# Gated linear attention with a feed-forward stage: the first nine units load groups of four tokens in long runs and turn them with 64-column products

## The chip, the cores and the metric

The kernel runs on one core of a Trainium2 chip. A core has a matrix engine (TensorE, PE in the profile, with PEld for its weight loads), a vector engine (VectorE, DVE), a scalar engine (ScalarE, ACT), a general engine (GpSimd, POOL) and a queue engine (SyncE, SP), which here issues all DMA transfers of data. PE writes its results to the accumulator memory PSUM, of which a bank holds 512 fp32 numbers per partition; all other data on the chip lies in SBUF with 128 partitions. The metric is the device time of one execution in microseconds (us); lower is better.

## What is computed

Two layers one after the other. First gated linear attention: for 4 batches, 8 heads, 768 tokens and 48 channels a head, a state of 48x48 is scaled by alpha row by row, gets the product of k and v added, and is read by q. Its output, 3072 tokens of 384 channels, goes through a feed-forward layer with 2048 hidden channels and a leaky maximum. All is fp32, except the two weight matrices, which arrive as float64.

```python
# q, k, v, alpha: (4, 8, 768, 48); alpha between 0.8 and 1.0
state = np.zeros((B, H, D, D), dtype=np.float32)
for t in range(S):
    state = alpha[:, :, t, :, None] * state + np.einsum('bhd,bhe->bhde', k[:, :, t], v[:, :, t])
    y[:, :, t] = np.einsum('bhd,bhde->bhe', q[:, :, t], state)
x = np.ascontiguousarray(y.transpose(0, 2, 1, 3)).reshape(B * S, H * D)   # 3072 x 384
h = x @ w_in                                                            # 384 x 2048
g = np.maximum(0.01 * h, h)
out = (g @ w_out).astype(np.float32)                                     # 2048 x 384
```

## The kernel before

**Units.** The 768 tokens are cut into 6 blocks of 128, and a *unit* is one block of one batch: 24 units, the block the slow index and the batch the fast one, so that units 0 to 3 are the first block of the four batches and carry no state in. The feed-forward layer takes three units at a time (`UPB = 3`). The first nine units, `AHEAD = 9`, run ahead of it; the other 15 are woven into it.

**One unit.** For the products the channels of two heads have to lie on partitions, 48 of one head at partition 0 and 48 of the other at 64 (`HB = 64`), and the 128 tokens along the row; four such pairs of heads make 512 columns, a bank of PSUM. alpha is turned into this layout and multiplied up along the tokens by a scan (`pc`, L309, one scan per pair); from the reciprocals of pc at every sixteenth token (L311) a second scan, backwards over all 512 columns, makes `rc` (L315). q times pc is `qs` (L334), k times rc is `ks` (L342). Eight products give the scores (L351); ACT copies them out (L361) and POOL zeroes the part above the diagonal (L362). ks is turned back to tokens on partitions (L374, copied by ACT, `ktok`). The outputs are products with the state (only from the second block on, units 4 and later) and with v (both L390); `kv` (L411) is what the unit adds to the state, copied by ACT for the first block (L430) or added to the state by DVE (L432). ACT and DVE split the outputs into two reduced-precision fp32 halves, high (L419) and low (L420), the input of the feed-forward layer.

**How the first nine units load and turn.** `load` puts tokens on partitions (`by_token`): each packet is the 48 channels of one token and head, 192 bytes, and a load of 192 KB has 1024 of them. alpha of unit 0 is loaded as two halves. A row then holds 8 heads at a pitch of 64, of which 48 are data; the gaps of 16 are filled with ones once, by DVE, at the start. `transposed` makes four PE transposes of 128x128 out of it (L272, against the unit matrix `ident`), one per pair of heads, into a whole bank. Later units load groups of four tokens, 768 bytes, and are turned by DVE in 32x32 blocks (L284); that stays as it is. There are two buffers each for alpha, q and k and three for v, so a load for unit u + 2 is issued when unit u has been turned.

**Order.** The program is written as a loop over units, in which `attention` interleaves the parts of unit u and of unit u + 1 (scans of u + 1; scores, mask and turned k of u; q and k of u + 1; outputs and state of u). Within the dependences the order on each engine is chosen by a scheduler from its own estimate of times; `tc.issue_after` ties single instructions to others. The PSUM banks of attention are two rings of three, `a` and `b`. PE keeps busy at the start with fillers, products of no use (`keep_warm`, L162, and `keep_warm_wide`, L167, which reads a tile of zeros): six ahead of everything, and some behind the turns of unit 0.

**Weights.** They arrive as 64-bit words in `raw` buffers on the same SP queue (L202, L206; the first two are tied to the v loads of units 4 to 7) and are converted by ACT and DVE into two fp32 halves (L237 to L257). The first of these jobs on ACT (L238) stands in ACT's order among the work of units 4 and 5; the conversions proper begin after ks of unit 7. With the feed-forward products (L487 in, L512 out, each a sum of three products of halves) PE is then supplied to the end.

## Time and profile before

| | |
|---|---|
| time, three runs | median 538.94 us (538.92 to 539.31) |
| profiled execution | 538.77 us, its span 537.1 us |
| PE busy | 518.8 us, 97% of the span; mean granted clock 0.991 |
| DVE, ACT, POOL busy | 375.0 us (70%), 234.0 us (44%), 49.1 us (9%) |
| instructions | 10383 |
| DMA | 92985 packets, 46.67 MB; 57856 of the packets under 512 bytes |

An engine's busy time is the time in which it executes; waits, and the issuing of transfers, are not in it. The span runs from the first to the last instruction. The granted clock is the share of full speed that the power throttle allowed PE. Most of the packets, and nearly all those under 512 bytes, are loads of attention; of 24 units' loads of v all are in 192-byte runs, of alpha, q and k those of the first nine units.

### The profile page before, as it was taken

The numbers are of one execution on the slowest core, as the hardware profiler recorded it, in microseconds if no ns is written. First come the engines' busy times: TensorE is split into PE (matmuls) and PEld (weight loads), VectorE is DVE, ScalarE is ACT, GpSimd is POOL, SyncE is SP. The second block draws the span as 40 slices with busy tenths as digits, with TensorE's granted clock in tenths as the row PEclk, the third lists the DMA queues.
The fourth block names the chain that finished last, engine by engine and source line by source line (L and its number), as shares of the span: only waits on it lengthen the run. The fifth ranks groups of instructions, "written<-read, shape, count | busy, mean of one in ns | idle before, by whom it ended". The sixth has DMA issues, their size and how long they took to land.

```text
span 537.1 us, 10383 instructions
## 1 busy us (share of the span) xinstructions
PE 518.8 (97%) x3934; PEld 492.6 (92%) x3934; DVE 375.0 (70%) x703; ACT 234.0 (44%) x514; POOL 49.1 (9%) x116
## 2 busy tenths in 40 slices
PE   8879899999999999999999999999999999999995
PEld 7668789999999899999999999999999999999995
DVE  6778999999988897875675685775777534332331
ACT  2665755555533453435334443344343354233331
POOL 3333510000000011010000001000000000000000
PEclk9999899999999999999999999999999999999998
DMA  9999854454823643533323422523201010001001
GB/s 149 163 179 183 198 140 119 117 131 136 183 53 87 190 117 78 107 81 98 70 67 70 108 69 64 98 50 92 71 0 38 11 35 1 22 1 45 1 1 49
DMA packets 92985, 46.67 MB, mean 87 GB/s; under 512 B 57856, under 2 KB 90112, under 8 KB 92928
## 3 DMA queue, kind: packets, MB, share of 16 engines
q1 hardware_dynamic: 92928, 45.93, 39.0%
q8 instruction: 33, 0.54, 0.4%
q14 instruction: 24, 0.20, 0.1%
HBM read 38.83 MB, written 4.72 MB: 81 GB/s over the span
## 4 chain that ended last, share of the span: by engine, by line
PE 86%; DVE 4%; DMA 3%; issue 2%; ACT 1%; SPq 1%; POOL 1%; ACTq 0%; DVEq 0%; POOLq 0%
PE ph L487 36%; PE b L512 32%; PE a L390 5%; PE a L351 4%; PE a L512 4%; DMA small<-in_alpha_dram 2%; DMA raw<-in_moe_w_in_dram 1%; PE a L374 1%; PE b L272 1%; PE a L411 1%; PE b L390 1%; DVE pc L309 1%; PE b L411 1%; POOL sm L362 1%; DVE rc L315 0%
## 5 line engine op out<-in xcount | busy, mean ns | idle before, releaser
L487 PE MATMUL ph<-large,w 128*128 128x384 f32 x1152 | 227.4, 340 | 2.8 <-DVE t L493 2.8
L487 PEld LDWEIGHTS ph<-large,w 128*128 128x128 f32 x1152 | 201.9, 189 | 5.5 <-DVE t L493 3.9
L512 PE MATMUL b<-w,gh 128*128 128x384 f32 x672 | 170.0, 340 | 0.0
L493 DVE TENSOR_TENSOR t<-ph,t 128x384 f32<-128x384 f32 x128 | 70.5, 551 | 88.7 <-ACT t L490 88.4
L512 PEld LDWEIGHTS b<-w,gh 128*128 128x128 f32 x672 | 119.7, 188 | 2.2 <-issue 0.5
L490 ACT ACTIVATE t<-ph 128x384 f32<-128x384 f32 x128 | 62.6, 489 | 130.1 <-PE ph L487 122.8
L495 ACT CAST gh<-t 128x384 fp32r<-128x384 f32 x128 | 65.7, 514 | 112.8 <-DVE t L493 102.6
L512 PE MATMUL b<-w,gl 128*128 128x384 f32 x336 | 107.4, 336 | 0.0
L499 DVE TENSOR_TENSOR gl<-t,gh 128x384 fp32r<-128x384 f32 x128 | 70.8, 553 | 34.4 <-ACT gh L495 33.2
L512 PEld LDWEIGHTS b<-w,gl 128*128 128x128 f32 x336 | 62.5, 188 | 0.1
L362 POOL TENSOR_SCALAR_AFFINE_SELECT sm<-sm 128x512 f32<-128x512 f32 x33 | 22.8, 705 | 113.3 <-ACT sm L361 113.3
L351 PE MATMUL a<-qs,ks 48*128 48x128 f32 x312 | 30.9, 287 | 0.1
L351 PEld LDWEIGHTS a<-qs,ks 48*128 48x128 f32 x312 | 25.9, 189 | 5.4 <-issue 4.4
L284 DVE STREAM_TRANSPOSE ks<-small 128x512 f32<-128x512 f32 x15 | 16.6, 1121 | 12.3 <-PE a L374 12.3
L390 PE MATMUL a<-sm,small 128*48 128x128 f32 (+1 forms) x312 | 23.2, 282 | 0.1
L319 POOL COPY pe<-pc 128x4 f32<-128x4 f32 x24 | 4.8, 202 | 188.6 <-DVE pc L309 188.6
L309 DVE TENSOR_TENSOR_SCAN pc<-e,small 128x128 f32<-128x128 f32 x60 | 20.1, 398 | 0.5 <-ACT pc L327 0.5
L367 POOL TENSOR_TENSOR small<-us,pe 112x192 f32<-112x192 f32 x20 | 11.9, 594 | 90.2 <-DVE us L432 87.5
L390 PEld LDWEIGHTS a<-sm,small 128*48 128x48 f32 (+1 forms) x312 | 17.1, 132 | 3.2 <-issue 3.0
L361 ACT COPY sm<-a 128x512 f32<-128x512 f32 x24 | 14.0, 585 | 13.8 <-PE b L351 11.1
L512 PE MATMUL a<-w,gh 128*128 128x384 f32 x96 | 20.0, 336 | 0.0
L315 DVE TENSOR_TENSOR_SCAN rc<-e,small 128x511 f32<-128x511 f32 x15 | 19.0, 1270 | 0.2
(86 smaller groups left out, 525.4 us busy)
## 6 DMA issues: line engine op xcount, KB each, us to landing
raw<-in_moe_w_out_dram SPq DMA_DIRECT2D x16, 384.0 KB, 3.9
small<-in_v_dram SPq DMA_DIRECT2D x24, 192.0 KB, 4.0
raw<-in_moe_w_in_dram SPq DMA_DIRECT2D x32, 144.0 KB, 3.9
out_dram<-t SPq DMA_DIRECT2D x24, 192.0 KB, 1.9
small<-in_alpha_dram SPq DMA_DIRECT2D x32, 96.0 KB, 2.3
small<-in_q_dram SPq DMA_DIRECT2D x30, 96.0 KB, 2.2
small<-in_k_dram SPq DMA_DIRECT2D x30, 96.0 KB, 2.2
small<-in_alpha_dram SPq DMA_DIRECT2D x30, 80.0 KB, 2.3
```

The lines of the kernel that those rows point to most:

```text
L284: nc.vector.transpose(t.rearrange("r p (j t) -> r p t j", t=T4), src.rearrange("r p (t d) -> r p t d", t=T4)[:, :, :, 0:32],)
L309: nc.vector.tensor_tensor_scan(pc[:, p, :], aT[:, p, :], ones.broadcast_to([P, C]), 1.0, ALU.mult, ALU.mult)
L315: nc.vector.tensor_tensor_scan(flat[2][:, NP * C - 2::-1], flat[0][:, NP * C - 1:0:-1], flat[1][:, NP * C - 2::-1], last, ALU.mult, ALU.add)
L351: nc.tensor.matmul(ss[s][:, p, :], ks[lo:lo + D, p, :], qs[lo:lo + D, p, :], start=True, stop=True)
L362: nc.gpsimd.affine_select(out=sm[s], in_=sm[s], compare_op=ALU.is_ge, fill=0.0, base=0, pattern=[[0, NP], [1, C]], channel_multiplier=-1)
L390: nc.tensor.matmul(y[s][HB * c:HB * c + lhsT.shape[-1], p % 2, :], lhsT, rhs, skip_group_check=True, **kw)
L487: nc.tensor.matmul(ph, w_in_of(f, wn, g), xt[:, g, :], start=n == 0, stop=n == 3 * NG - 1)
L490: put(ordered, "ACT", lambda: nc.scalar.mul(t, ph, 0.01))
L493: put(ordered, "DVE", lambda: nc.vector.tensor_tensor(t, ph, t, ALU.max))
L495: put(ordered, "ACT", lambda: nc.scalar.copy(gh, t))
L499: made["gl", i, f] = put(ordered, "DVE", lambda: nc.vector.tensor_tensor(gl, t, gh.bitcast(F32), ALU.subtract))
L512: nc.tensor.matmul(po[j], gt[:, js], w_out_of(f, wn), start=f == 0 and n == 0, stop=f == NF - 1 and n == 2)
```

## The change

For the first nine units alpha, q and k come in one transfer each with runs of four tokens, 768 bytes, 256 of them per load. Partition j*4 + p of the buffer gets group j (four tokens) of the head pair p, and the two heads of the pair (the *halves*, s) lie behind each other in the row at the pitch of 208. What before was the transpose of a pair of heads is now, for each of the four tokens n of a group and for each half s, a product of 64 columns of the buffer with `turn`, a unit matrix whose columns are permuted so that pairs come out as the slow and groups as the fast index. A product's result is 64 partitions by 128 columns; it goes to the half's partitions (0 to 63 or 64 to 127) and to every fourth column of the bank, from n on. So a tensor takes eight products, two for each of the four tokens, in place of four transposes. The gaps that are filled at the start become one run of 16 behind each half (by DVE) and the rest of the row (by POOL); `turn` is made by POOL with one copy from `ident`. The two halves of alpha's first load become one transfer, and the wide fillers and their tile of zeros are gone: q's, k's and alpha's turns of unit 0 each have two plain fillers behind the second and the fourth token.

```diff
--- before.py
+++ after.py
@@ -83,8 +83,8 @@
             parts.append(part)
         return parts
 
-    ident, mask, ones, acc, seed, *rest = pieces(
-        "small", F32, (P,), (C,), (1,), (2 * NU,), (NP, C), *[(NP * D,)] * B, *[(DM,)] * NV, *[(NP * PITCH,)] * sum(NL)
+    ident, turn, mask, ones, acc, seed, *rest = pieces(
+        "small", F32, (P,), (P,), (C,), (1,), (2 * NU,), (NP, C), *[(NP * D,)] * B, *[(DM,)] * NV, *[(NP * PITCH,)] * sum(NL)
     )
     state, vals_sb, rest = rest[:B], rest[B:B + NV], rest[B + NV:]
     loads_sb = [[rest.pop(0) for _ in range(n)] for n in NL]
@@ -123,11 +123,10 @@
         ts = slice(tb * C, (tb + 1) * C)
         t, src = loaded(u, i), (alpha, q, k)[i]
         if u < AHEAD:
-            n = H if u or i else H // 2
-            for h in range(0, H, n):
-                nc.sync.dma_start(
-                    by_token(t)[:, h:h + n, 0:D], src[b, h:h + n, ts, :].rearrange("h t d -> t h d")
-                )
+            nc.sync.dma_start(
+                t[:, 0:2 * PITCH].rearrange("r (s n) -> r s n", s=2)[:, :, 0:RUN],
+                src[b, :, ts, :].rearrange("(p s) (j t) d -> j p s (t d)", s=2, t=T4),
+            )
             return
 
         for a in range(4):
@@ -151,8 +150,6 @@
 
     nc.vector.memset(seed, 0.0)
     nc.vector.memset(ones, 1.0)
-    zeros = cst.tile([P, 4 * C], F32R, name="zeros")
-    nc.gpsimd.memset(zeros.bitcast(F32), 0.0)
 
     idle = ps_h.tile([P, 512], F32, name="ph")
 
@@ -161,21 +158,20 @@
         for _ in range(n):
             nc.tensor.matmul(idle[:, 0:C], seed[:, 0, :], seed[:, 1, :], start=True, stop=True)
 
-    def keep_warm_wide(n):
-
-        for _ in range(2):
-            nc.tensor.matmul(idle[:, 0:n], zeros[:, 0:P], zeros[:, 0:n], start=True, stop=True)
-
     keep_warm(6)
+    def tails(t):
+        return t[:, 0:2 * PITCH].rearrange("r (s n) -> r s n", s=2)[:, :, RUN:]
+
     for i in (0, 1, 2):
         for t in loads_sb[i]:
-            nc.vector.memset(by_token(t)[:, :, D:], 1.0)
+            nc.vector.memset(tails(t), 1.0)
     for n in range(max(NL)):
         for i in range(3):
             if n < NL[i]:
                 load(n, i)
         load_values(n)
     make_identity(nc, ident)
+    nc.gpsimd.tensor_copy(turn.rearrange("r (p j) -> r p j", p=NP), ident.rearrange("r (j p) -> r p j", p=NP))
     nc.gpsimd.memset(mask, 1.0)
     nc.gpsimd.affine_select(
         out=mask, in_=mask, compare_op=ALU.is_ge, fill=0.0, base=0,
@@ -183,7 +179,7 @@
     )
     for i in (0, 1, 2):
         for t in loads_sb[i]:
-            nc.gpsimd.memset(t[:, H * HB:], 1.0)
+            nc.gpsimd.memset(t[:, 2 * PITCH:], 1.0)
 
 
     runs = [(0, D, 0, 1, D), (D, GAP, NG * D, NG, 1), (HB, D, NP * D, 1, D), (BR, GAP, (NP + NG) * D, NG, 1)]
@@ -267,18 +263,17 @@
 
         src = loaded(u, i)
         if u < AHEAD:
-            ps = banks4()
-            for p in range(NP):
-                last = nc.tensor.transpose(
-                    ps[:, p, :], by_token(src)[:, 2 * p:2 * p + 2, :].rearrange("t h d -> t (h d)"), ident
-                )
-                if u == 0 and p % 2:
+            ps = bank()
+            for n in range(T4):
+                for s in (0, 1):
+                    at = s * PITCH + n * D
+                    last = nc.tensor.matmul(
+                        ps[HB * s:HB * (s + 1), n::T4], src[:, at:at + HB], turn, start=True, stop=True, skip_group_check=True
+                    )
+                if u == 0 and n % 2:
                     with tc.issue_after(last.ins):
-                        if i == 2:
-                            keep_warm_wide(4 * C if p == 1 else 2 * C)
-                        else:
-                            keep_warm(2)
-            return ps
+                        keep_warm(2)
+            return ps.rearrange("r (p t) -> r p t", p=NP)
         t = atp.tile([P, NP, C], F32, name=name, **kw)
         src = src.rearrange("r (p n) -> r p n", p=NP)[:, :, 0:RUN]
         nc.vector.transpose(
```

The order that the scheduler makes of it changes as well. On SP, which issues the transfers, the start of the program stood like this (`in_alpha_dram`, `in_q_dram`, `in_k_dram` and `in_v_dram` are the inputs):

```order
L128 DMA small<-in_alpha_dram 128x4x48 x2
L128 DMA small<-in_q_dram 128x8x48
L128 DMA small<-in_k_dram 128x8x48
L128 DMA small<-in_alpha_dram 128x8x48
L128 DMA small<-in_q_dram 128x8x48
L128 DMA small<-in_k_dram 128x8x48
L147 DMA small<-in_v_dram 128x8x48 x3
```

and now:

```order
L146 DMA small<-in_v_dram 128x8x48 x2
L126 DMA small<-in_alpha_dram 128x2x192
L126 DMA small<-in_q_dram 128x2x192
L126 DMA small<-in_k_dram 128x2x192
L126 DMA small<-in_alpha_dram 128x2x192
L126 DMA small<-in_q_dram 128x2x192
L126 DMA small<-in_k_dram 128x2x192
L146 DMA small<-in_v_dram 128x8x48
```

The first two loads of v have moved ahead of the first alpha.

On PE, one cycle of the early units from the turned-back k of a unit u on (the L272 behind it are q and k of unit u + 1, the lone one further down is alpha of unit u + 2):

```order
L374 MATMUL a<-small,ks 128x112 x4
L272 MATMUL b<-small 128x128 x4
L272 MATMUL a<-small 128x128 x4
L390 MATMUL b<-sm,small 64x128
L390 MATMUL b<-sm,small 48x128
L390 MATMUL b<-sm,small 64x128
L390 MATMUL b<-sm,small 48x128
L272 MATMUL b<-small 128x128 x4
L411 MATMUL b<-small,ktok 64x48
```

and the same cycle now, with the lines moved up by some four or five (L369 is the former L374, L270 the turns, L385 the former L390, L406 the former L411):

```order
L369 MATMUL a<-small,ks 128x112 x4
L270 MATMUL a<-small 64x128 x2
L270 MATMUL b<-small 64x128 x8
L270 MATMUL a<-small 64x128 x6
L385 MATMUL b<-sm,small 64x128
L385 MATMUL b<-sm,small 48x128
L385 MATMUL b<-sm,small 64x128
L385 MATMUL b<-sm,small 48x128
L270 MATMUL b<-small 64x128
L406 MATMUL b<-small,ktok 64x48
```

The first of alpha's eight products stands where all of alpha's transposes stood; its other seven have moved behind the kv products (L406) and the second half of the outputs, right ahead of the next scores.

On DVE, one unit of the early ones (the `x` halves, L420, belong to the unit before the one whose scans stand around them):

```order
L309 SCALAR_TENSOR_TENSOR pc<-b,small 128x128 x4
L310 MEMSET b 128x32
L420 TENSOR_TENSOR large<-b,large 112x2x128
L311 RECIPROCAL small<-pc 128x32
L420 TENSOR_TENSOR large<-a,large 112x2x128
L315 SCALAR_TENSOR_TENSOR rc<-b,small 128x511
L334 TENSOR_TENSOR qs<-b,pc 128x512
L342 TENSOR_TENSOR ks<-a,rc 128x512
```

and now (L415 is the former L420, L304 the scans over pc, L310 the scan over rc, L329 and L337 qs and ks):

```order
L415 TENSOR_TENSOR large<-a,large 112x2x128
L415 TENSOR_TENSOR large<-b,large 112x2x128
L304 SCALAR_TENSOR_TENSOR pc<-b,small 128x128 x4
L305 MEMSET b 128x32
L306 RECIPROCAL small<-pc 128x32
L310 SCALAR_TENSOR_TENSOR rc<-b,small 128x511
L329 TENSOR_TENSOR qs<-b,pc 128x512
L337 TENSOR_TENSOR ks<-a,rc 128x512
```

Both x halves of the unit before have moved ahead of the scans. (The names of the operations are the program's; the profile calls the scans TENSOR_TENSOR_SCAN.)

## The prediction

> **What bounds the kernel now.** I read the page, then busy time by stage, then the timeline of the first 60 us, since the change touches only units 0 to 8.
>
> ```profile
> span 537.1 us, 10383 instructions
> PE 518.8 (97%) x3934; PEld 492.6 (92%) x3934; DVE 375.0 (70%) x703; ACT 234.0 (44%) x514; POOL 49.1 (9%) x116
> PE ph L487 36%; PE b L512 32%; PE a L390 5%; PE a L351 4%; PE a L512 4%; DMA small<-in_alpha_dram 2%; DMA raw<-in_moe_w_in_dram 1%; PE a L374 1%; PE b L272 1%; PE a L411 1%; PE b L390 1%; DVE pc L309 1%; PE b L411 1%; POOL sm L362 1%; DVE rc L315 0%
> ```
>
> The span is 537.1 us of an execution of 538.77 us; the median of the runs is 538.94, 0.17 above. The chain is PE's. By stage (start:end, length, then busy time of PE, PEld, DVE, ACT, POOL, then the granted clock):
>
> ```profile
> 51.09:76.41 25.32, 22.74 (x234) 19.62 (x231) 24.16 (x42) 14.26 (x32) 9.19 (x11) 0.93 0.77 173
> 76.41:537.10 460.69, 453.05 (x3192) 436.61 (x3192) 312.18 (x568) 192.98 (x416) 22.82 (x56) 1.00 0.30 73
> ```
>
> From 76.41 on PE is full (453.05 of 460.69), and nothing there is edited. From 51.09, where ks of unit 7 is done, to 76.41 DVE is full (24.16 of 25.32) with weight conversions. So the end moves by as much as ks of unit 7 moves, less what DVE's 1.2 us of idle time can take back. What sets that moment is the pace of units 0 to 7, from one score product (L351) to the next:
>
> ```profile
> 5.69 1.36 DVE L309 TENSOR_TENSOR_SCAN pc<-a,small 128x128 f32<-128x128 f32 x4 [3.36 <-PE a L272]
> 10.00 0.37 PE L351 MATMUL a<-qs,ks 48*128 48x128 f32 x1
> 16.08 0.37 PE L351 MATMUL a<-qs,ks 48*128 48x128 f32 x1
> 32.92 0.37 PE L351 MATMUL a<-qs,ks 48*128 48x128 f32 x1
> 41.50 0.58 PE L351 MATMUL a<-qs,ks 48*128 48x128 f32 x1
> 47.13 0.37 PE L351 MATMUL a<-qs,ks 48*128 48x128 f32 x1
> ...
> 50.41 0.68 DVE L342 TENSOR_TENSOR ks<-a,rc 128x512 f32<-128x512 f32 x1
> ```
>
> These are the scores of units 0, 1, 4, 5 and 6 and the last ks: 6.08 us for unit 0, (32.92-16.08)/3 = 5.61 for units 1 to 3, 8.58 for unit 4, 5.63 for unit 5, then 3.96 to 51.09. Unit 4 is long because ACT, in order, waits for weights:
>
> ```profile
> ACT raw L238 <- DMA raw<-in_moe_w_in_dram: 2.6, 1, 2.6
> 30.95 2.84 SPq L202 DMA_DIRECT2D raw<-in_moe_w_in_dram  x4
> 37.14 0.66 PE L272 MATMUL b<-small 128*128 128x128 f32 x4 [1.99 <-ACT us L430]
> 39.10:42.50 3.40, 3.40 (x40) 3.31 (x39) 3.17 (x8) 1.37 (x5) 0.37 (x2) 0.50 1.30 148
> ```
>
> After 1.99 us without work PE also gets half the clock (0.50) for 3.4 us.
>
> **The change part by part.** *Transfers.* 192-byte packets become 768-byte ones. Two stretches, packets, MB, share of the 16 engines, of 12 us from 6 and of 9 us from 138:
>
> ```profile
> q1 hardware_dynamic: 10741, 2.03, 142.6%
> q1 hardware_dynamic: 2425, 1.52, 68.4%
> ```
>
> 192 KB in the first kind take 12 x 0.197/2.03 = 1.16 us of a full queue. In the second, with 640- and 768-byte packets, 9 x 0.684 x 0.197/1.52 = 0.80 if 100% is full and 0.56 if 142.6% is; I take 0.65. So 27 loads free some 13 us of transfer time. That would pay only where a unit waits for data: unit 0, unit 2 (1.24 us in unit 0's 6.08) and the weights of unit 4.
>
> *Order on SP.* Both v loads now stand ahead of the first alpha. Issues and landings (start and length; then, in the chain, a load from issue to landing):
>
> ```profile
> 0.82 0.99 SPq L128 DMA_DIRECT2D small<-in_alpha_dram  x2
> 3.03 4.60 DMA small<-in_alpha_dram
> small<-in_alpha_dram SPq DMA_DIRECT2D x1, 96.0 KB, 2.4
> small<-in_alpha_dram SPq DMA_DIRECT2D x1, 96.0 KB, 2.7
> ```
>
> The two halves land at 3.2 and 4.0, and alpha of unit 1, three loads later, at 7.63: (7.63-4.0)/3 = 1.2 each, in order of issue. So v of unit 0 lands at 4.0, of unit 1 at 5.2, and alpha at 5.85: 1.85 later than now. Bounds: 0 later if the queue let it pass, 2.0 later with 0.80 per load. I take the queue, since every landing shows it. POOL's new turn table is ready by then: its fills of 416 instead of 320 columns add 0.6 us, the copy perhaps 0.4, the dropped zeros give back 0.5, and they ended at 4.0. SP's waits for DVE's fills of the gaps end before the v issues do. q and k land 0.65 apart, ahead of their turns.
>
> *Turns.* Four transposes become eight 64-column products. Rows of one unit:
>
> ```profile
> 11.09 0.60 PE L374 MATMUL a<-small,ks 112*128 112x112 f32 x4
> 11.53 0.60 PE L272 MATMUL b<-small 128*128 128x128 f32 x4
> 11.97 0.60 PE L272 MATMUL a<-small 128*128 128x128 f32 x4
> 12.56 0.65 PE L390 MATMUL b<-sm,small 128*64 128x128 f32 x8
> ...
> 15.04 0.61 PE L411 MATMUL b<-small,ktok 128*64 128x48 f32 x15
> ```
>
> Four transposes are 4 records: 11.97-11.53 = 0.44, 0.11 a step. L390's four 64-column fp32 products are 8 records (two per product) and take 0.65, no more than four steps and the last one's 0.27: neighbours of different column halves run side by side. A tensor is then 16 records in 8 steps, 0.87 instead of 0.44. Bounds: 0.44 if a step could be halved, 1.74 if the halves did not pair. I take 0.87; L390 is the same shape. Per unit that is 3 x 0.43 = 1.3 us more on PE, which waits about 1.4 of each 5.61 us now, so the cover is just used up.
>
> *Pace.* From a score product: 1.53 to the turns (10.00 to 11.53); q and k 1.74, 3.27; L390 waits for rc, which frees its bank: the scan can start 0.25 after the scores and rc ends about 3.1 later, 3.4; four L390 0.44; the first of alpha's products, alone, 0.22; L411 and the other L390 1.04 (15.04 to 16.08); seven products 0.87. That is 5.95; I take 5.9, and 5.8 for unit 0, where that wait is nil. Units 4 and 5 have state products besides:
>
> ```profile
> 50.06 0.32 PE L390 MATMUL b<-qs,small 48*64 48x128 f32 x2
> ...
> 50.67 0.66 PE L272 MATMUL b<-small 128*128 128x128 f32 x4
> ```
>
> 0.61 more, while the wait for rc disappears and the alpha product is no longer alone: 6.2. DVE stays below: from the scan at 9.86 to the end of ks at 14.18 are 4.32, with L420 twice 5.05.
>
> ```profile
> 9.86 1.35 DVE L309 TENSOR_TENSOR_SCAN pc<-b,small 128x128 f32<-128x128 f32 x4
> 13.50 0.68 DVE L342 TENSOR_TENSOR ks<-a,rc 128x512 f32<-128x512 f32 x1
> ```
>
> DVE now does L420 ahead of the scan, so it waits for the two casts; but they end with L411, just before alpha's products, which the scan needs anyway: nothing. The old loop over us, state scaling and masks (5.61) falls away.
>
> *Sum.* Alpha 5.85; its products and two fillers to the scan 7.5 (now 5.69); reciprocal 9.3; the six fillers that wait for it (0.22 each), k's last product, two fillers and alpha of unit 1 take 3.0: scores of unit 0 at 12.3 instead of 10.0. Then 18.1, 24.0, 29.9, 35.8, 42.0, 48.2, and ks of unit 7 4.7 later (4.32, the state sum and a short wait) at 52.9 instead of 51.09. Unit 4's stall is gone in this: its weights follow v of unit 5, free at 28.9 instead of 30.0, and land near 33.5, where ACT comes at 33.8; if they take as long as now, up to 1 us returns. So +2.3 at the start, -0.3 unit 0, +0.9 units 1 to 3, -2.4 unit 4, +0.6 unit 5, +0.7 for the last step: +1.8. DVE's waits after 51 take back some 0.4: +1.4, or 538.77+1.4 = 540.2, 540.3 on the median's scale. The wide fillers were PE's waiting time; dropping them costs nothing.
>
> **Rivals.** Under 0.2% (1.08 us) nothing can be told from no change, so the bounds are 537.9 and 540.0.
>
> *Slow products.* Nine products of 384 columns at full rate (start, length):
>
> ```profile
> 76.41 1.83 PE ph L487 x9
> ```
>
> A step might double because results go into every fourth column, or the halves might not pair; no row writes PSUM with gaps. L390's pairs speak against the second. Price 2.6 us a unit over seven, 1.5 at the start: +20, 558 to 560. The Trainium skill, PSUM — Partial Sum Buffer, Specifications, says of PSUM's 8-byte cache lines that "any non-contiguous AP slows matmuls significantly"; by that rule this case would be the forecast, and no run here shows it yet. I hold it less likely since an fp32 step already takes 0.11 us for 128 columns while L487's wider ones take 1.83/9 = 0.20 for 384, so each column has time to spare.
>
> *Half clock at the start.* PE idles from 4.46 (end of the first fillers) to 5.85, 1.4 us. If that costs a 3.4 us window as in unit 4, the PE-bound piece before 12.3 takes 0.9 to 2.9 longer: 542.2. It decides if such a gap, 1.4, is enough; 1.99 was, and the 1.24 us wait for unit 2's alpha was not. The Trainium skill, TensorE: Matmul & The Clock Gate, Part 1, wants one whole idle window of about 3.4 us; by it this case cannot happen, but the trace's 1.99 disagrees.
>
> *No delay at the start.* If alpha passes the v loads it lands at 4.2, and 1.65 us come back: 538.6, no change. Against it is the even spacing of landings.
>
> *PE not the bound: faster.* If a 64-column product took half a step, PE would need 4.6 and DVE's 5.05 (5.35 with state) would set the pace: 0.85 x 5 units and 0.6 at the start, 4.9 in all: 535.3. It wins from a pace of 5.5 down. Against it, L390's steps.
>
> **How the numbers follow.** Forecast 51%, own range 538.6 to 542; no delay 17%; half clock 14%; slow products 10%; faster 8%. The range 536.9 to 543.6 leaves out the slow products and most of the fast case. Faster: 8, 5 from the forecast's lower edge, 4 from no delay: 17%. Same: 16 and 13: 29%. Slower: 30, 14 and 10: 54%.
>
> **What would show it.** Alpha's first product at 5.9 and the scores of unit 0 at 12.3; L270 in 8 steps of 0.11; score products 5.9 and 6.2 apart with PE never long idle; no long ACT wait for raw; ks of unit 7 near 52.9. I am wrong if the pace falls under 5.6, a step differs from 0.11, or alpha lands before 5.

## The result and the profile after

The changed kernel takes 545.10 us (median of four runs, 544.01 to 545.55) against 539.12 (538.92 to 539.53) for the kernel before: ratio 1.0104, 95% interval 1.0082 to 1.0127, so it is 6 us slower. The forecast had the sign right and the size wrong: 540.3, with a range that ended at 543.6.

The page of the execution after (545.24 us, its span, the busy times, the chain and the packets):

```profile
span 543.4 us, 11011 instructions
PE 530.6 (98%) x4262; PEld 505.3 (93%) x4262; DVE 375.3 (69%) x703; ACT 235.9 (43%) x514; POOL 49.1 (9%) x116
PE ph L482 36%; PE b L507 32%; PE a L385 5%; PE a L346 5%; PE a L507 4%; PE b L270 2%; PE a L270 2%; PE a L369 1%; DMA small<-in_alpha_dram 1%; PE a L406 1%; PE ph L159 1%; PE b L385 1%; DVE pc L304 1%; DMA raw<-in_moe_w_in_dram 1%; PE b L406 1%
DMA packets 72234, 46.69 MB, mean 86 GB/s; under 512 B 30192, under 2 KB 69360, under 8 KB 72176
```

The transfers did what the change says: 27,664 fewer packets under 512 bytes. PE has 328 more records (an fp32 product has two) and 11.8 us more busy time; DVE, ACT and POOL are busy for as long as before within 2 us. From the timeline (start, length, engine, line), the scores of units 0, 1, 4, 5 and 6 and ks of unit 7, which answer to the rows at 10.00, 16.08, 32.92, 41.50, 47.13 and 50.41 of before:

```profile
15.46 0.37 PE L346 MATMUL a<-qs,ks 48*128 48x128 f32 x1
21.30 0.37 PE L346 MATMUL a<-qs,ks 48*128 48x128 f32 x1
38.84 0.37 PE L346 MATMUL a<-qs,ks 48*128 48x128 f32 x1
45.44 0.37 PE L346 MATMUL a<-qs,ks 48*128 48x128 f32 x1
51.91 0.37 PE L346 MATMUL a<-qs,ks 48*128 48x128 f32 x1
55.72 0.68 DVE L337 TENSOR_TENSOR ks<-a,rc 128x512 f32<-128x512 f32 x1
```

And by stage (length, busy PE, PEld, DVE, ACT, POOL, granted clock, DMA share, GB/s):

```profile
15.46:21.30 5.84, 5.84 (x102) 5.41 (x100) 4.75 (x11) 3.44 (x9) 1.54 (x4) 1.00 0.41 113
38.84:45.44 6.60, 6.60 (x117) 5.81 (x116) 5.37 (x14) 3.82 (x11) 2.05 (x5) 1.00 0.96 232
56.40:81.66 25.26, 22.40 (x268) 19.50 (x263) 24.25 (x42) 14.20 (x31) 7.21 (x9) 1.00 0.52 131
81.66:85.10 3.44, 3.44 (x11) 3.44 (x12) 3.41 (x6) 2.98 (x6) 0.00 (x0) 0.50 0.72 212
85.10:543.40 458.30, 451.06 (x3183) 434.64 (x3181) 308.77 (x563) 192.00 (x411) 23.87 (x56) 1.00 0.29 72
```

In units 0 to 6 PE is busy for all of the time (5.84 of 5.84, 6.60 of 6.60): the cover is used up. The conversions take as long as before (25.26 against 25.32). Behind them there is something new, 3.4 us at half clock. Term by term, in us:

| from | forecast | measured |
|---|---|---|
| start, to the scores of unit 0 | +2.3 | +5.46 |
| unit 0 | -0.3 | -0.24 |
| units 1 to 3 | +0.9 | +0.70 |
| unit 4 | -2.4 | -1.98 |
| unit 5 | +0.6 | +0.84 |
| unit 6, to the end of ks of unit 7 | +0.7 | +0.53 |
| from there to the end | -0.4 | +0.99 |
| sum, of spans | +1.4 | +6.30 |

Two terms miss, the first and the last. The start in the timeline, where the alpha transfer's row is start and length of the issue:

```profile
1.93 0.82 SPq L126 DMA_DIRECT2D small<-in_alpha_dram  x1
5.59 1.12 PE L270 MATMUL a<-small 128*64 128x128 f32 x8 [1.12 <-DMA small<-in_alpha_dram]
...
8.96 1.37 DVE L304 TENSOR_TENSOR_SCAN pc<-a,small 128x128 f32<-128x128 f32 x4 [7.24 <-PE a L270]
10.00 1.09 PE L270 MATMUL b<-small 128*64 128x128 f32 x16
```

Eight records of the turns take 1.12 us at 5.59 and sixteen take 1.09 at 10.00, so PE runs at half speed until about 10. (The granted clock of the views has no record of the start and reads 1.00 there; its first record, the full clock, begins at 9.98.) In the kernel before, it begins at 4.97, between two turns of the same size:

```profile
4.25 0.64 PE L272 MATMUL a<-small 128*128 128x128 f32 x2
5.27 0.38 PE L272 MATMUL a<-small 128*128 128x128 f32 x2
```

### The profile page after: what moved, and what is told of

It is laid out like the page before. It is cut to its first block, busy times and chain, and to the rows that moved or that the text cites. A ratio compares the mean times of both kernels' runs of the same rounds, so it can differ in the third digit from the quotient of the medians.

```text
span 543.4 us, 11011 instructions
## 1 busy us (share of the span) xinstructions
PE 530.6 (98%) x4262; PEld 505.3 (93%) x4262; DVE 375.3 (69%) x703; ACT 235.9 (43%) x514; POOL 49.1 (9%) x116
## 4 chain that ended last, share of the span: by engine, by line
PE 90%; DVE 4%; DMA 2%; issue 1%; ACT 1%; SPq 1%; POOL 1%; ACTq 0%; DVEq 0%; POOLq 0%
PE ph L482 36%; PE b L507 32%; PE a L385 5%; PE a L346 5%; PE a L507 4%; PE b L270 2%; PE a L270 2%; PE a L369 1%; DMA small<-in_alpha_dram 1%; PE a L406 1%; PE ph L159 1%; PE b L385 1%; DVE pc L304 1%; DMA raw<-in_moe_w_in_dram 1%; PE b L406 1%
## 5 line engine op out<-in xcount | busy, mean ns | idle before, releaser
L385 PE MATMUL a<-sm,small 128*64 128x128 f32 (+1 forms) x312 | 23.5, 278 | 0.4 <-POOL sm L357 0.4
L385 PEld LDWEIGHTS a<-sm,small 128*64 128x64 f32 (+1 forms) x312 | 17.3, 129 | 3.6 <-issue 3.0
L304 DVE TENSOR_TENSOR_SCAN pc<-e,small 128x128 f32<-128x128 f32 x60 | 20.0, 394 | 0.0
L270 PE MATMUL b<-small 128*64 128x128 f32 x272 | 19.9, 276 | 0.0
```

The costliest lines, as they stand in the source:

```text
L270: last = nc.tensor.matmul(ps[HB * s:HB * (s + 1), n::T4], src[:, at:at + HB], turn, start=True, stop=True, skip_group_check=True)
L304: nc.vector.tensor_tensor_scan(pc[:, p, :], aT[:, p, :], ones.broadcast_to([P, C]), 1.0, ALU.mult, ALU.mult)
L385: nc.tensor.matmul(y[s][HB * c:HB * c + lhsT.shape[-1], p % 2, :], lhsT, rhs, skip_group_check=True, **kw)
```

## The experiments

Rows that begin with a time are from the timeline, rows with an arrow from the view of waits, rows with two times from the view by stretches of time.

The theory: PE starts every execution at half clock and gets the full one only after some 3.4 us of work (from 1.53 to 4.97 in the kernel before); the late alpha left it idle for 1.1 us in that time, and so the half clock lasted until 9.98. The main rival: only the late landing itself and the turns' own time count. (The medians of some kernels below spread by several us, and the last section says what goes with it; where a step is to be told, I use the rows of the profiled executions.)

**Order on SP alone.**

```diff
     for n in range(max(NL)):
-        load_values(n)                       # inside the loop of loads
+        with behind("l", max(NL) - 1, 2):    # behind k of unit 1; v of unit 2 likewise
+            load_values(n)
```

> The changed kernel with one edit: all loads of v wait on SP behind the sixth load of alpha, q and k, as they stood before. Theory (the late alpha leaves PE idle, so its clock stays at half until 10 us, and the half clock is most of the 5.5 us by which the scores of unit 0 come late): alpha lands near 3.5 instead of 5.5, PE has no gap at the start, the clock is full from about 5, the first scan starts near 6.3 (8.96 in the changed kernel, 5.69 before) and the scores of unit 0 near 11.3 (15.46 and 10.00); the end moves by as much, to about 541.0. Rival one (only the 1.9 us of the late landing count, the clock is no matter): scores of unit 0 near 13.4, about 543. Rival two (the half clock belongs to the new products and not to the gap): the clock is still half until 10, the scores come no earlier than 14, about 544.

Measured: ratio 1.0091 (1.0059 to 1.0123), profiled execution 541.56 us. Scores of unit 0:

```profile
13.21 0.37 PE L348 MATMUL a<-qs,ks 48*128 48x128 f32 x1
```

2.25 us earlier than in the changed kernel, and near what rival one said. The start went wrong for every theory: the order took v out of the way, but alpha's issue waited for DVE's fills and began at 1.55, so alpha landed at 4.62 and not at 3.5; PE still had a gap, of 0.3 us, and full clock came at 6.7. This run cannot tell the clock from the landing.

**More fillers alone.** `keep_warm(6)` becomes `keep_warm(10)`; alpha lands as late as in the changed kernel.

> The changed kernel with one edit: ten fillers ahead of everything in place of six, so that PE stays busy until alpha, still late, lands at 5.5. Theory (the gap of PE costs the clock): full clock between 5 and 7 instead of 10, first scan near 7.4, scores of unit 0 near 12.5 instead of 15.46, about 542.2. Rival (the late landing is the cost, not the clock): scores still at 15 or later, no gain, 545 or more.

Measured: ratio 1.0099 (1.0068 to 1.0130), profiled execution 543.37 us. The turns of alpha and the scores of unit 0:

```profile
5.72 0.66 PE L270 MATMUL a<-small 128*64 128x128 f32 x8
13.29 0.37 PE L346 MATMUL a<-qs,ks 48*128 48x128 f32 x1
```

The same eight records now take 0.66 us instead of 1.12, though they start 0.1 later, and the scores come 2.17 us earlier. Nothing but useless products was added, and the full clock begins at 5.26. So 2.2 us of the start are the clock, somewhat below the 3.0 expected.

That the gap made it holds with one condition. The clock changes only on a grid of 3.41 us, whose place differs between executions (last section). In the changed kernel the step of this grid from 3.16 to 6.57 held the gap, PE was busy for 2.29 us of it, and the full clock came a step later. Two kernels below start with the same six fillers and the same gap of 1.1 us: with neighbouring columns the step from 2.68 to 6.10 held the gap, was busy for 2.28 us, and the full clock came at 9.51; with products not paired the step that mattered, 1.25 to 4.66, ended almost as the gap began, was busy for 2.93 us, and the full clock came at 4.66. So the gap costs a step where the grid puts the gap inside one, as in the changed kernel's profiled execution, and not in every execution.

In the ratios this gain can't be told: those of the order edit, of these fillers and of both together have intervals that overlap that of the changed kernel. Of executions with a mean clock of 0.999, the changed kernel's took 544.01 us, the one with these fillers 542.93.

**Both.** The order edit and eight fillers.

> Both edits of the two runs before, with eight fillers. Theory: if alpha's early landing closes the gap by itself, the two more fillers only stand in the way: within 0.5 us of the run with the order alone, about 541. Rival (a gap is left in that run): 0.5 to 1.5 us better than it.

Measured: ratio 1.0082 (1.0052 to 1.0111), profiled execution 542.93 us.

```profile
12.50 0.37 PE L348 MATMUL a<-qs,ks 48*128 48x128 f32 x1
```

0.7 earlier than with the order alone, as the rival had it, but not for its reason, the gap of 0.3 us. With the order alone the step from 3.31 to 6.72, gap and all, was busy for 3.12 us and was followed by full clock; the step before it had ended ahead of the gap. The run with old turns below has the same order edit, six fillers and a gap of 0.3 us, and its full clock begins at 4.82. So these 0.7 us are where the grid fell.

Of the 5.46 us at the start, 2.2 are the clock and 0.8 the late alpha (13.29 less 12.50: in both runs alpha's products begin at full clock, at 5.72 and 4.93); 2.5 are left. Two rows of this run, PE's fillers and ks of unit 0, show where:

```profile
9.93 2.05 PE L159 MATMUL ph<-small 128*128 128x128 f32 x16
10.44 0.68 DVE L339 TENSOR_TENSOR ks<-a,rc 128x512 f32<-128x512 f32 x1
```

ks ends at 11.12, 1.17 later than in the kernel before (9.95), and the scores wait another 1.38 for PE, where before they began 0.05 behind ks. What stands in front of them is the eight fillers behind the turns of q and k, products of no use, and the rest of alpha of unit 1. A run without these fillers was not made.

**New turns with old transfers.** Loads by token in 192-byte runs, with the order edit:

```diff
-                t[:, 0:2 * PITCH].rearrange("r (s n) -> r s n", s=2)[:, :, 0:RUN], ...
+                by_token(t)[:, :, 0:D], src[b, :, ts, :].rearrange("h t d -> t h d")
```

> New turns, old transfers: the order edit as in the first run, and alpha, q and k loaded in 192-byte runs by token as before, one transfer each; the turns read the columns of the new layout, so the output is not that of the reference. Theory (the turns make PE the bound at 5.85 us a unit, and the long runs pay only at unit 4): units 1 to 3 stay at 5.85, unit 4 takes 8 us or more again because ACT waits for the weights, and the whole is about 2 us slower than the first run, 543. Rival one (the transfers are worth nothing): as the first run, 541. Rival two (192-byte loads also stop units 1 to 3, since the queue is full): units above 6 us, 545 or more.

Measured: ratio 1.0090 (1.0060 to 1.0120), profiled execution 544.14 us, no difference in time that the runs could tell from the order edit. Scores of units 4 and 5 from the timeline, and ACT's wait from the view of waits (in total, times, longest):

```profile
35.92 0.37 PE L345 MATMUL a<-qs,ks 48*128 48x128 f32 x1
44.37 0.37 PE L345 MATMUL a<-qs,ks 48*128 48x128 f32 x1
ACT raw L233 <- DMA raw<-in_moe_w_in_dram: 2.3, 1, 2.3
```

Units 1 to 3 stay at 5.85, as theory and PE's full time say, and unit 4 takes 8.45. With these turns, 192-byte runs cost nothing in units 1 to 3, and some 1.5 us in unit 4 (8.45 against 6.84 with the order edit alone and 7.07 with fillers besides).

**New transfers with old turns.** The order edit, and four transposes of neighbouring columns:

```diff
-                for s in (0, 1):
-                    ...
+                last = nc.tensor.transpose(ps[:, n * C:(n + 1) * C], src[:, n * C:(n + 1) * C], ident)
```

> New transfers, old turns: the order edit as in the first run, and four transposes of 128 neighbouring columns in place of the eight products. They take the wrong columns, so the output is not that of the reference; the cost on PE is that of the kernel before. Theory (the turns make PE the bound at 5.85 us a unit): PE waits again, the pace of units 1 to 3 falls to 5.0 to 5.4 us, where DVE's 5.05 set it, units 5 and 6 to 5.6, ks of unit 7 starts near 48.5 instead of 53.7, and the time is about 537 (541.5 in the profiled run of the order edit). Rival one (waits between the engines hold the pace as before, whatever the transfers): 5.6 us, ks of unit 7 near 50.5, 538.5. Rival two (PE is not the bound): 5.85 us, 541 or more.

Measured: ratio 0.9983 (0.9964 to 1.0002), profiled execution 537.70 us. Scores of units 3, 4 and 5, and ACT's wait:

```profile
24.97 0.37 PE L344 MATMUL a<-qs,ks 48*128 48x128 f32 x1
29.85 0.37 PE L344 MATMUL a<-qs,ks 48*128 48x128 f32 x1
39.32 0.37 PE L344 MATMUL a<-qs,ks 48*128 48x128 f32 x1
ACT raw L236 <- DMA raw<-in_moe_w_in_dram: 2.1, 1, 2.1
```

The pace falls to 4.88, below the 5.05 that I had taken for DVE's. So PE's turns are what holds the changed kernel at 5.85. That the other 0.7 us, against before's 5.61, is the worth of the long runs does not follow. In units 1 to 3 of the kernel before the view of waits has no engine waiting for a load. It has a wait of ACT that this run does not have: in each of the three units the copy of the scores waits for POOL's scaling of the state (total, times, longest):

```profile
ACT sm L361 <- POOL small L367: 2.0, 3, 0.7
```

The run with long runs for units 4 and 5 alone, below, does not have it either, and takes 5.01 and 5.00 us for units 1 and 2, although the data turned in unit 1 came in 192-byte runs. So 0.7 us a unit is likely the scheduler's order on ACT and POOL; no run tells apart what the transfers add. Unit 4 takes 9.47 here, ACT waits again for weights that are issued behind v of unit 5, and most of the gain is lost there.

**Products not paired.** The loops over s and n swapped.

> The changed kernel with the loops over halves and tokens swapped, so that four products into partitions 0 to 63 come one after another, then four into 64 to 127. Theory (products into different halves run side by side only next to each other): 16 steps of 0.11 instead of 8, 1.75 us a tensor, 2.6 us more a unit, pace 8.4 us, about 563. Rival (the pairs cost nothing less than single ones: what is seen is the rate of 64 columns): no change, pace 5.85, 545.

Measured: 549.01 us, one run; paces of units 0 to 3 6.45, 6.95, 6.74 and 6.73. Theory and rival both miss. The turns of q and the beginning of k of one unit:

```profile
22.54 0.65 PE L270 MATMUL a<-small 128*64 128x128 f32 x4
23.03 1.20 PE L270 MATMUL b<-small 128*64 128x128 f32 x13
24.07 0.27 PE L270 MATMUL b<-small 128*64 128x128 f32 x1
24.12 0.27 PE L270 MATMUL a<-small 128*64 128x128 f32 x1
```

From 24.07 on products of the two tensors start 0.05 apart in turn: the second half of one tensor ran beside the first half of the next, so of q and k three stretches of eight records are left where the theory had four. That they pair is shown (8 more steps of 0.11 are the 0.88 us by which the pace rose); they need not be neighbours in the program.

**Neighbouring columns.** `ps[..., n::T4]` becomes `ps[..., n * C:(n + 1) * C]`.

> The changed kernel with one edit: each product writes 128 neighbouring columns instead of every fourth. The tokens come out in another order, so the output is not that of the reference; the number and size of all instructions stay. Theory (columns with gaps cost nothing; a step is the 0.109 us of the product itself): L270 still 16 records in 0.87 us, pace of units 1 to 3 still 5.85. Rival (gaps in PSUM slow the product): a step under 0.09, the pace under 5.6, PE with waits again, 2 us or more faster than 545.

Measured: 544.63 us, one run; paces of units 0 to 3 5.85, 5.84, 5.85 and 5.85. A turn in this kernel, then one in the changed kernel:

```profile
16.89 1.09 PE L270 MATMUL b<-small 128*64 128x128 f32 x16
```

```profile
17.08 1.09 PE L270 MATMUL b<-small 128*64 128x128 f32 x16
```

Every fourth column costs nothing in this one run. The Trainium skill, PSUM — Partial Sum Buffer, Specifications, has any access that is not contiguous slow a product down; for fp32 at a stride of 16 bytes the two rows disagree.

**Long runs for units 4 and 5 alone**, in the kernel before (`if u in (4, 5)` ahead of both old paths).

> The kernel before with the new loads and turns for units 4 and 5 alone. Theory (long runs pay where the weights of unit 4 wait in the queue, and the turns cost 1.3 us of PE a unit, which unit 4 has to spare): the weights land 2 us earlier, unit 4 takes 6.5 to 7 us instead of 8.6, PE has no gap of 2 us there, unit 5 near 6; ks of unit 7 starts near 48.7 instead of 50.4, about 1.5 us faster than the kernel before. Rival one (ACT's order is the stall, not the queue): unit 4 stays at 8.5, 0.5 us slower than before. Rival two (units 4 and 5 pay the 0.8 us each that units 5 and 6 paid in the changed kernel): the gain is used up, within 0.5 us of before.

Measured: ratio 1.0018 (0.9998 to 1.0038). Unit 4 takes 8.97 us and ACT waits 2.5 for its weights, as rival one said. The weights do land earlier, at 34.35 instead of 36.00, but units 1 and 2 take 5.0 us here and ACT comes as much earlier, at 31.8 instead of 33.4. So the stall is the time between ACT's coming and the landing, and shorter transfers alone did not close it.

**Fillers in the gap of unit 4**, in the kernel before: `keep_warm(5)` behind the turned-back k of unit 4.

> The kernel before with five fillers on PE behind the turned-back k of unit 4, where PE waits 2 us for ACT. Theory (PE's gaps of 1.5 us and more cost a window of 3.4 us at half the clock): the gap falls to 0.9, the clock stays full at 39 us, the scores of unit 5 come up to 1.2 us earlier, about 0.8 us faster in the median. Rival one (the gap is not what lowers the clock): half clock there as before, same time. Rival two (the fillers delay unit 4): 0.3 to 1 us slower.

Measured: ratio 1.0006 (0.9991 to 1.0021). Unit 4 fell to 7.69 and there was no half clock in the profiled execution (mean 0.998 against 0.991), so the clock was about 0.9 of the 8.58 us of unit 4. The time is the same: ks of unit 7 starts at 50.46 (50.41 before), since the scores of unit 0 came 0.4 later, with a full clock that began at 5.81, and the step from unit 6 took 0.5 longer. The theory's mechanism holds and its gain doesn't.

**Work ahead of the wait near 80 us**, in the kernel with order and eight fillers:

```diff
+                for _ in range(6 if i == 1 and f == n == j == 0 else 0):
+                    nc.tensor.matmul(po[j], gt[:, js], w_out_of(f, wn), start=True, stop=True, ...)
                 nc.tensor.matmul(po[j], gt[:, js], w_out_of(f, wn), start=..., stop=...)
```

> The run with the order edit and eight fillers, and six repeats of the first output product of the second group of units (L507's first of i = 1, f = 0, each overwriting the one before), so that PE has work just ahead of the 1.9 us in which it waits for DVE near 80 us. Theory (that wait costs a window of half clock, 1.7 us of PE): the wait shrinks to about 0.9, there is no half clock near 80, and from the start of ks of unit 7 to the end are 486.1 us instead of 487.9; 1 to 1.7 us faster than the same kernel without the repeats. Rival (the clock falls there for another reason): half clock there as before, no faster.

Measured: ratio 1.0054 (1.0033 to 1.0074), profiled execution 542.16 us, mean clock 0.997 to 0.998 in all six runs, where the kernel without the repeats had 0.993 to 0.999. PE's wait ahead of the half clock, in the changed kernel and here:

```profile
PE ph L482 <- DVE t L488: 1.9, 1, 1.9
```

```profile
PE ph L484 <- DVE t L490: 0.9, 1, 0.9
```

The 3.41 us before and after that moment in the changed kernel, then here:

```profile
78.25:81.66 3.41, 1.48 (x9) 1.16 (x7) 3.31 (x5) 1.23 (x3) 0.00 (x0) 1.00 0.12 23
81.66:85.07 3.41, 3.40 (x11) 3.41 (x12) 3.38 (x6) 2.95 (x6) 0.00 (x0) 0.50 0.72 214
```

```profile
76.55:79.96 3.41, 2.51 (x14) 2.19 (x14) 3.34 (x6) 1.19 (x4) 0.00 (x0) 1.00 0.37 103
79.96:83.37 3.41, 3.41 (x22) 3.41 (x21) 3.41 (x7) 2.59 (x5) 0.00 (x0) 1.00 0.56 132
```

The half clock is gone, as the theory says; since the order edit and two more kernels also had none there, the six mean clocks say more than the one row. The gain is smaller than it said: from ks of unit 7 to the end 487.2 us, where the same kernel without the repeats had 487.9 and the order edit, without a half clock there though its PE waits 1.8 us, 486.1. The repeats are work of PE themselves.

**ACT's first weight job later**, in the kernel before:

```diff
-        with nullcontext() if lines["ACT"] else behind("hi", f - 1):
+        with nullcontext() if lines["ACT"] else behind("hi", f - 1) if f else behind("xh", 5):
```

> The kernel before with one edit: ACT's first weight job (L238, f = 0) stands behind its casts of unit 5 instead of among the work of unit 4. Theory (unit 4's 8.6 us are ACT's in-order wait for weights that nobody needs before 51 us): unit 4 takes about 6, PE has no gap of 2 us and no half clock at 39, ks of unit 7 starts near 48 instead of 50.4. The end comes at most 2.4 us earlier, about 1.5, 537.4. Rival (what follows ks of unit 7 is set by the weights or by PE and not by it): ks near 48, the end within 0.5 us of before.

Measured: 536.66 us against 539.96 on the same chip, ratio 0.9946 (0.9929 to 0.9963): faster than both kernels. Scores of units 4 and 5, and ks of unit 7:

```profile
33.19 0.37 PE L351 MATMUL a<-qs,ks 48*128 48x128 f32 x1
38.61 0.37 PE L351 MATMUL a<-qs,ks 48*128 48x128 f32 x1
48.71 0.68 DVE L342 TENSOR_TENSOR ks<-a,rc 128x512 f32<-128x512 f32 x1
```

Unit 4 takes 5.42 instead of 8.58. All that the transfers gained in unit 4 of the changed kernel was to be had by one tie on ACT.

**All mends on the changed kernel**: order, eight fillers, ACT's job, the repeats.

> The changed kernel with every mend: v behind the loads of alpha, q and k, eight fillers, ACT's first weight job behind the casts of unit 5, six repeats of an output product near 80 us. Theory (what is left is the products' time on PE: 1.3 us at the start, 0.23 a unit for units 0 to 3, 0.8 for units 4 to 6): ks of unit 7 starts near 52.8 against 48.7 in the kernel before with the same mend of ACT, no half clock near 80, about 540.0, 0.3% slower than before. Rival (ACT's wait was hiding the rest): unit 4 near 6, ks of unit 7 under 51, 538 or less.

Measured: ratio 1.0066 (1.0040 to 1.0092), profiled execution 541.49 us, ks of unit 7 at 53.36. Against the run above, with the same edit on ACT, that is 4.65 us at ks of unit 7: 2.47 at the start (12.55 against 10.08), -0.39 unit 0, 0.71 units 1 to 3, 1.05 unit 4, 0.61 unit 5, 0.20 the last step. The two spans, 539.8 and 534.3, differ by 5.5. The theory's moment for ks was near (52.8), its terms less so (1.3 at the start, 0.9 for units 0 to 3, which are 0.32), and its time 1.5 us too short. With the clock and the order mended, the 1.98 us of units 0 to 5 are what the products cost on PE. The 2.47 at the start are more than that: alpha's first product begins at 4.99 instead of 4.25, and the fillers behind q and k hold the scores up here too.

**New transfers, old turns, ACT's job later.**

> New transfers, four transposes of 128 neighbouring columns (the wrong ones, so the output is not that of the reference), and ACT's first weight job behind the casts of unit 5. Theory (with cheap turns the short transfers are worth 0.6 to 0.7 us a unit, and ACT's wait hid it): the pace of units 1 to 3 stays 4.9, unit 4 takes about 5.3 instead of 9.5, ks of unit 7 starts near 43.5, about 533 to 534. Rival (behind ks of unit 7 PE or the weights are the bound): ks near 43.5, but the time within 1 us of the kernel before with the same mend of ACT (0.9946 of before), 536 or more.

Measured: 535.18 us, ratio 0.9918 (0.9890 to 0.9946); ks of unit 7 at 44.96, unit 4 at 5.41. One unit:

```profile
25.80:30.68 4.88, 4.79 (x66) 3.92 (x65) 4.68 (x12) 3.71 (x11) 2.02 (x5) 1.00 0.76 188
```

Between theory and rival, nearer the rival: ks of unit 7 is 3.75 us earlier than with ACT's job alone, the time 1.5 (0.28%, intervals overlap). So even with turns for nothing little would be left of the change: PE with 4.79 of 4.88 us and DVE with 4.68 are full there, and the pace may be that of the order on ACT and POOL, since ACT's wait for POOL's scaling is missing here too. Where the rest of the 3.75 us went behind ks of unit 7 was not tried; in its profiled execution one step of half clock stood at 72.

**POOL spreads the runs**: three copies a unit of 128x512 into a tile with the halves 64 apart, then four transposes with `turn` into every fourth column; order and ACT's job as above.

> New transfers and turns of one step: POOL copies each load from the 768-byte runs into a tile in which the two halves of a token stand 64 apart, so that four transposes of 128 columns (with the permuted unit matrix, into every fourth column) do a tensor's turn; loads of alpha, q and k ahead of v on SP, and ACT's first weight job behind the casts of unit 5. The output is that of the reference. Theory (the eight products were what the change cost, ACT's wait is what is left): the pace of units 1 to 3 is 4.9 to 5.2 as with the four transposes of neighbouring columns, unit 4 near 5.5, ks of unit 7 starts near 44, about 533. Rival (POOL's three copies a unit, 0.5 us each, stand ahead of the masks, and its scaling of the state): pace 5.6 to 6, ks near 49 to 51, 538 or more.

Measured: 545.86 us, ratio 1.0121 (1.0088 to 1.0154). The profiled execution took 552.37, with half clock from 48.99 to 76.30; the unit shown lies ahead of that. Pace and time are the rival's, but POOL, 3.84 of 5.89 here, is not what is full:

```profile
21.44:27.33 5.89, 5.86 (x66) 4.98 (x65) 4.91 (x11) 3.70 (x11) 3.84 (x9) 1.00 0.58 139
```

PE, with as few records as in the run above (66), is busy for 5.86. In the order of its instructions the scheduler had put the four scores of bank b behind each other and then those of bank a, where other kernels have them in turn.

**The same with the scores in turn**: each score tied behind the one before.

> The run with POOL's copies, with one edit: the eight score products of a unit are held in the order in which they are written, the two banks in turn (in that run the scheduler put four of one bank behind each other, and PE was busy 5.85 of 5.88 us a unit). Theory (those did not run side by side, about 0.9 us a unit): the pace of units 1 to 3 falls to 5.0, ks of unit 7 starts near 44.5, about 534, faster than the kernel before with ACT's job moved. Rival (POOL's copies set the pace: 3.85 us of POOL a unit between scans and masks): pace 5.5 or more, 538 or more.

Measured: ratio 1.0026 (1.0011 to 1.0041).

```profile
26.99:31.79 4.80, 4.78 (x67) 4.02 (x65) 4.65 (x12) 3.59 (x11) 3.83 (x9) 1.00 0.78 194
50.67:54.08 3.41, 1.07 (x16) 0.87 (x16) 3.34 (x5) 2.83 (x6) 0.93 (x1) 1.00 1.23 228
57.49:64.33 6.84, 6.06 (x51) 5.21 (x49) 6.74 (x10) 2.18 (x4) 1.36 (x3) 0.50 0.18 35
```

The theory is right on the pace, 4.80: the order of eight products was worth 1.1 us a unit, and POOL's copies hide. It is wrong on the time: units 4 to 6 take 6.82, 5.68 and 6.28, ks of unit 7 starts at 49.01, and then PE is busy for 1.07 of 3.41 us and works at half clock for 10 us. What delays units 4 to 6 was not tried.

## Why the prediction was wrong

**The bound and the pace: right.** A tensor's turn is 16 records in 0.87 us as forecast, the score products stand 5.84 apart where 5.9 were forecast, PE has no waits left, unit 4's stall is nearly gone. One reading behind it was off: PE was said to wait 1.4 us of each 5.61, and the view by stretches has it busy for 4.79, so it waits 0.82. The pace was summed from rows and not from this, and came out right. Units 4 and 5 were put at 6.2 and take 6.60 and 6.47. I had let the state products remove the wait for rc and pair alpha's lone product; PE is busy throughout, so there was no wait left to remove.

**The start: the step that failed.** Alpha's landing (5.46 for 5.85) was fair, and from there on I counted PE's work at full clock. The half clock stood among the rivals at 14% and 542.2, and I held against it that a wait of 1.24 us in mid-run had not cost anything, and a rule for losing the clock. Neither bears on it: they say when a PE at full clock keeps it, and at the start PE is at half clock and has yet to get the full one. The rows that did were in the trace of before: its clock turns full at 4.97, 3.4 us after the first filler at 1.53, with no gap between. With the gap filled 2.2 us came back, within the 0.9 to 2.9 that the rival had; in an execution with the grid elsewhere the forecast may have been off by less. A further 1.0 was undersized PE work, most of it between the first scan and the scores: in the run with fillers alone that takes 5.63 us (7.66 to 13.29), in the forecast 4.8, and PE is busy for all of it. The forecast had six of the eight fillers begin as the reciprocal ends (9.42 there); PE was then still at k's turns, went on to alpha of unit 1, and began the fillers at 10.73.

**The end: a term that was missing.** Forecast were 0.4 us back from DVE's waits behind ks of unit 7. The conversions gave back next to nothing (25.26 for 25.32), and behind them PE waited 1.9 us for DVE where it had waited 0.9 before, and a step of half clock followed: +0.99 instead of -0.4. From the start of ks of unit 7 to the end are 486.7 us in the kernel before, 486.1 to 486.4 in three runs without that half clock (order alone, products not paired, neighbouring columns) and 487.7 to 487.9 in the four with it (the changed kernel, fillers, both, old transfers). So the forecast gain was there, and the half clock cost 1.3 to 1.8 us more than it. Why PE's wait there doubled is open. The prediction knew half clock behind a wait from unit 4 of the kernel before, and asked for it at the start only.

**The rivals.** Slow products: no (the kernel with neighbouring columns). No delay from v: no, alpha's later landing was worth 0.8. PE not the bound: no; but where the turns are cheap the pace is 4.88, so that rival's price was about right and only its condition failed.

## What to carry to other kernels

Before PE's turns are doubled to make transfers shorter, ask what the transfers hold up: here it was one stall, which a single tie on ACT removed (0.9946) at no cost. Where an engine is busy for 85% of a unit, its last waits are a budget, and 1.3 us of new work in 5.6 spends it all. When a first transfer is delayed, check that the fillers reach to its landing, and that fillers further on do not stand in front of work that is ready.

## What the runs showed of the clock

The granted clock changes on a grid of 3.413 us, whose place in the program differs between executions: in the kernel before at 4.97, 39.10 (10 steps later) and 59.58 (16 steps), in the changed kernel at 9.98 and 81.66 (21 steps). A step in which PE was busy for little of the time can be followed by one at half clock. Of the order edit:

```profile
78.40:81.81 3.41, 2.14 (x12) 2.14 (x13) 3.38 (x6) 2.10 (x4) 0.00 (x0) 1.00 0.70 217
81.81:85.22 3.41, 3.41 (x22) 3.41 (x21) 3.41 (x7) 1.23 (x3) 0.00 (x0) 1.00 0.08 19
```

PE waits 1.8 us near 80 here too, but the grid cuts the wait in two; the busy share of the step is 0.63, and the clock stays. In the changed kernel the share was 0.43, and it fell. Over the profiled executions, of the steps at full clock ahead of the last 10 us, all eight with a share of 0.31 to 0.53 were followed by half clock, of nine with 0.54 to 0.61 only three, and from 0.63 on only two (0.66 and, in the first run with POOL's copies, 0.81). At the start 0.59 to 0.67 were not enough to get the full clock, and 0.85 was. So a low share brings the fall, but between about a half and two thirds something else decides, and that is open; so is why, in that run, PE stayed at half clock for eight steps in which it was busy throughout. The Trainium skill, TensorE: Matmul & The Clock Gate, Part 1, asks for a whole idle window for the fall; these rows disagree, the step of the changed kernel that was 0.43 busy was enough.

The medians spread with it. One step at half clock takes 0.5 x 3.41/540 = 0.003 from an execution's mean clock, and of the kernel with the order edit the three runs at 0.999 took 541.46 to 541.66 us, the five at 0.992 to 0.996 543.6 to 547.4. That the place of the grid is most of the difference between two runs of one program is likely, but was not shown: only one execution of each kernel has rows.
